# A gated attention and spectral mix on one core: another order list for all engines, another sequence of the last head groups

## The chip, the cores and the metric

The kernel runs on one core of one Trainium2 chip. The metric is device time in microseconds of one execution. A core has five engines that are written here as PE (TensorE, matrix products), ACT (ScalarE), DVE (VectorE), POOL (GpSimd) and SP (the queue that issues most DMAs). Each engine runs its instructions strictly in the order of its own queue and waits on semaphores where an operand comes from another engine. PE writes to PSUM, which here is cut into one place of three banks (psA), one of two (psB), one accumulator (pv) and two single banks (bg).

## What is computed

```
def _A_ref(x, wqkv, wo):                       # B, S, D = 1, 2048, 448; H = 16, Dh = 28
    qkv = (x @ wqkv).reshape(B, S, 3, H, Dh).transpose(2, 0, 3, 1, 4)
    q, k, v = qkv[0], qkv[1], qkv[2]
    p = softmax(einsum("bhqd,bhkd->bhqk", q, k) * Dh ** -0.5)
    o = einsum("bhqk,bhkd->bhqd", p, v)
    return o.transpose(0, 2, 1, 3).reshape(B, S, D) @ wo

def _B_ref(x, w_r, w_i):                       # a spectral filter over (S, D)
    X = rfft2(x) * (w_r + 1j * w_i)
    return irfft2(X, s=(S, D)).astype(bfloat16)

g = sigmoid((x * gate_w).sum(-1, keepdims=True))
return g * _A_ref(x, wqkv, wo) + (1 - g) * _B_ref(x, w_r, w_i)
```

Full softmax attention over 2048 tokens and 16 heads, mixed token by token with a two-dimensional Fourier filter of the same input.

## The kernel before

**Tiling.** The 16 heads are four groups g of four heads, each head on one strip of 32 partitions (28 used). The queries are four blocks c of 512. A pair (g, c) is a round n; there are 16 rounds, and `self.groups` (plan_steps) gives their sequence: groups 0 and 1 in order of c, then the eight pairs of `LAST8` (line 31) for groups 2 and 3. Within a round the keys are 16 tiles kt of 128.

**Scores and exps.** A unit is one (round, key tile, head): a 128x512 score product on one row strip of PE. Units are taken three and two at a time (`WID`), alternately into psA and psB; one such step is one score operation on PE and one exp on ACT (line 953, in attention()), which writes bf16 into a ring of 25 slots, or for the first eight spare steps into a pd tile. There are 315 steps. A score needs its PSUM place back from the exp two steps earlier. Beside the exps, the last four key tiles of most rounds are not given to ACT: their scores (called dunit) go to a bg bank, DVE turns each into a bf16 approximation of an exponential by an integer conversion (line 988, "conv"), and three further copies at other phases are made with one integer addition (line 1000, "phase"), each either by DVE or by POOL. A pv product (four column-tiled matrix products into the accumulator pv) takes each key tile's result.

**Rounds.** After a round's last pv product DVE copies the accumulator out, two small DMAs and one large broadcast through DRAM (rs, rsc, Rb) bring the reciprocal of the softmax sum times the gate to all rows, and POOL multiplies (line 1080, in normalise()); the result lies in q, whose block is no longer needed. An output tile t of 128 tokens (out_tile()) sums four products of the inverse transform and four of wo, one for each group g, of q's block c = t // 4; a tile can be finished when all four groups have that block normalised. The last round has a shorter path of its own (last_norm(), lines 1090 to 1114), and tiles 12 to 15 end with it.

**Everything else** is woven between the steps: the transposes of x, the q, k and v projections (mm4(), four column-tiled products), the forward transform, the filter product and the inverse transform (background()), all through the two bg banks.

**The head.** head() loads x and the first q and k weights, spreads those weights into padded tiles wpq and wpk (ACT copies, line 494; the borders are set by POOL memsets, lines 480 to 484, in padset()), transposes x on PE (line 425), copies the result to xT (DVE line 559, ACT line 557), projects q and k, and adds a row with the squared norms. `NWARM` = 14 products of a zero tile (set by a POOL memset, line 514) run on PE ahead of and among the first transposes.

**What sets the order.** Every operation is an Op object with an engine, a function that emits its instructions, its dependencies, and figures for its duration (dur) and latency (lat). The kernel has no scheduler: plan() reads the order from a table, `PLAN`, and issue() emits in that order. PLAN has three parts, two of them compressed: a list of operation numbers for all engines together (a number of 60000 or more is a filler, a warming product of zeros, see filler()); one byte for each PSUM item and pd tile that says which bank or buffer it takes; and a list of those phase operations that run on DVE rather than POOL (alts). Each engine's queue is the list restricted to that engine. The framework puts semaphores where the data demand them; issue() adds one wait of its own, from a DVE operation marked lk to the next POOL operation in the list.

```
def plan(self):
    order, place, alts = PLAN
    order = np.frombuffer(zlib.decompress(base64.b85decode(order)), "<u2")
    place = np.frombuffer(zlib.decompress(base64.b85decode(place)), "u1")
    for it, b in zip(self.items, place):
        it.bank = int(b)
    for i in alts:
        self.ops[i].eng = "DVE"
    return [int(i) if i >= 60000 else self.ops[i] for i in order]
```

Of the kernel before, what the change touches and what calls it, by code (L numbers as in the profile page):

```python
# [20 lines left out]
S, D, H, DH, F = 2048, 448, 16, 28, 225  # L21
F2 = 2 * F
NT, P, C = 16, 128, 112
# [7 lines left out]
LAST8 = [(2, 0), (2, 1), (2, 2), (3, 0), (2, 3), (3, 1), (3, 2), (3, 3)]  # L31
# [6 lines left out]
TA, TB, BREL = 40, 300, 26.0  # L38
XREL, WREL = (0.0, 6.0, 11.0), 30.0
EARLY = 8  # L40
KA = 256
PLAN = (
    (
        'c-kG8Qx_Ok&;YM?@9y5%wr$(CZQHhO+qRP;wr#et+c?dKA24Sg=ZsQDf$}PbBBhm8F;y&uDz<V;6sw@(s0b>qil{29$SR(SqN1w!'
        'Dw?XK5~!N0txBl6tE8%;s-@bgL~5K$p+>62Dw0a3lBiB9x$3M^snjZsN~zMRv?_y2uQI8Os;bJYqN^;by{e+Jsvatv%C2&#d@85P'
        'rE;r0DzD0~3aEmrwrZ>jsiLZwDy)jDBC3QcsY<ERs;o+GQkrrqg{h;;sPbx#nycoi3TnPus1~WkYJpm!E~`}Lin^+<smZE|TB=f;'
        'DJre0r_z|~YMENDR;ZP#zj~+Mt5vFn`k>O8(dwgGt<sy-@{d}hTB;0YfXZmrsy(Wj+N<`d{c4?BD+g3&vtCtKnanx0L7i6@)J3&j'
        't&$yTr@EwesVpX|StGmEG&Nn#k{N2I>aCipY^IsYZU(77YO0#8`l^kpz8a+(s7<Panx%%Q9A>kcAzM^VQ&$aDTh%u8o2sFHS6$Q}'
        'Dwp|F&5_*Zpt_-EN*<Hf98xz`R5`2~s#YqQZ={B)Tk43)XKt%W>W<29=E)aTz<gCJ<*xds3Yyj`nzT{()OR&jCHIBQeO1`3kRR%V'
        'I;o17@#>WNSDjV^)lt=4olz52QIo<CR$bLG)lC&Q#mreXTzyh$eMhxi>dI$T!qk&7s=hRkpK63EX%@PMa$HSNDSauk$jx=7O)5Xn'  # L50
        '&39!?S+l?`cIo^Q_du01<;^npm-<^hRm<H&^-NVT70pZ4PbvLaY5hVO{Z?6B$y7E@XYkKe6;su$a7$fR=_V^(cX^|FNJd}H^pxsm'
        'olET>sr4?sf2C@enr4+-<5s&gKC^$VviP;GmZ@zvyHt9UORdxBI;O7K;x@RnI;&5ox4L?!zS-t7`4|#Y8klVUiE3zex{WTD>~gUs'
        'yD#r6`Z&_a%$CMxyQ|=LxUzn(q}NSMWxv}sH3wV<{hQ0E_qa^DnQ3nRbeVNQU%<C82VG0^yDQ}Px<A~1s*3-mTA9{npDW|{yQ)5m'
        'Zez0QZ2FKp>Dn65<@_nv&K!2_O?I7A=h8WJ2a{Xp(MMfJlUEn^MSUl8#C0}B{4rPCcQMCZS3~-QV=X%99KM@5?Yf%?x|T2Q&$t@C'
        'hv{jqxQP0kyXqq8$U2JdWqO+nE~+l(EBQX=qU&p}xwEdizwS_%@Fl(1{Y-yz$<_3iT{InC4=^$Gc{k9+*0)?t9Y+r`adj*mPY*Wn'
        'bqsUY4K+hdHGj{Q_9OI2eZwV^QF^o<W)jOySIQ4JV{{U^?M9jrrj8%1hv=dDjvJ<X_)%uK{@aZ<&HYo?*^e<V+*p%9kJaP!cs)Un'
        'Gvm!m*Hd-z6ZJDU!L;<x-77cIH1n@rS3k+zcau#_^Uh7ull2rm#XN9R^;_4?Pt#M)L)YEMGSkc>H{JB~u}xcvV`i9k^2Eh8Gfh0x'
        '!asKLO?&AevrIz$mz!-8>BKsT?kI2EKtIRy^GWqw^RH{|6PQn~m7ixmyToR``RKm5gr=<@;1`%g<{!7vymu*dZ~wtnm1>eqSC>U5'
        'pI&TI>i)ilEHQQc54Y6Rl<%&MZ|8ry{JMZHs0-<3ri3o6mz)1wQT^4G)GN&jlT?c7Z?3OTCVhMn{mUhn6q3`gGQCtT?_sq`DeXN$'
        'aUEcd>E$CpL|AJ&_&h!mbn@%Wdc%<0#}$FRKAyyv4JLu)^BawUD3DN+nvUK=a;;#K*=#hF)#Y?~y~R|}0M&I3T~k-o`F$<D)zsG8'  # L60
        '%{G%)@`-~%KED)@tg^#olY%nXXO|o@%P;adWvAI~5O$eNGR8-Ru|BiR_i1I1spqpu9N25pNnDui(@O@~XG-h+roPW8sU$Kq@Z)`I'
# [12 lines left out]
        'PHX6wp9{I{Wyx)4!AzJ93*eIEv6>dbHOXt|L7@3?LN3YyIVt&UetSx;$Zz5(0xf~7Qoyc;g7$Y=1AoXPi9(kClnYYG7Pc$lu{_eJ'
        'WfeTuPjnHxR6mrWb}1}^zw}?S45HH+iAE2knEhK9w~JvpJdv}q0!r9(5{d51c`0cJ>g#et)<a|}WlP%)a8uSoMDkR|Mx~gv5#Grb'
        'C~JY<%T|a%<?K4x1m*1@9g8a1igp`(l+BQYGSFMu4u8v2S*&AIC3{OM+h>xLZcAp0E*Ytc-3fc4s@)AbB%?i$g?`Bn$VAzwn%xKg'
        '$Zt^H{thbCur=*|NJ$_32YD_B;EtrA<n+<+g1hpMuVri7KjEqVPoC*I_PM?%HoVXWp{{+YPrw^VO((&GdiDs^w>ju29D^6qz<%+^'
        ';Se;me?XHLpZ#HYDgXLc(#STpap<SKmbCQApMfT}sXYs+=p6hjr{R;Nq0e#|n%U+y59OjO(85Lz=b@!N1?lMmxDYWw$VvGLLo3_b'
        'UW9b?McUX)kT~3cuW}RaKwBF%<fW?+CES8`w!O_ww;>-z3SWJ8>R|7}J?Ll?gsgNQ_UUNBhyA*fEkK=ZT>2*Q=(}8l($vK!30>_&'
        'C_@p#0ev01+3xm-Jc8eJDf(Uau+O2VeF1+#e5yqW=x?C#7<$>>Hc_ZUPv8M?kdTP_*qRhV!qC?~g}U?%qKEjQ9QCsW=^ga9uOUV#'  # L80
        'PYLNg46qI9B~+uNA!c|318rHVM}zEJNFP4HVEYPc&_~D^{(&KOsQnlI&>6y?`k+3fGlgOH6AZW2sWu(fpCMToVUvdjlp>6@UtyFT'
        'ZNEW*P>E88CRCZm*e_5hjI}@E7gV6k;Xg=B6{$Yu4+_WG@fOizmhc^7g$Z_|{Q<GV5q(r2(*}?0Np`X&JfSr<qQ=A+Crq(%LlsIF'
        ';)SW!VZqRp04)kmv(s%=3V2eV(lhL7-HguYnf9zs75Y;jnq|-F$T-_(4Si{j%@#US6pV;-Z3oI8Qin8Qo}F*|QQA-;oYx&`fz1&v'
        '=!^Q2E<_bWOk8LS(`B7A6rorc0T<cDHab=cT`2}e#j;_EU23CYu8=#F51lAa_@v8(Wp=rJrOO2|!F<*$Z3$XoBVhznj3OE^XbOkO'
        'CN_FQW|fU(iqmS#CJ7d$q`1bewRuAqii7#W5E@98LtLy9*4gzo0aguPbvNokQOpKAls4Lg*gC|+K~$3BWBZT@H`&cLF{Z{2p%+yP'
# [162 lines left out]
class Kernel:  # L248
# [250 lines left out]
    def head(self):  # L499
        nc = self.nc  # L500
        self.grp = "head"
        K0 = -5000.0
        self.pad_ms, self.wready, self.d_x, self.xev, self.xtr = {}, {}, [], {}, []
        dx = [self.dma(self.xtok[:, 2 * i:2 * i + 2, 0:D], self.x[:, 2 * i:2 * i + 2, :], (), K0 + i, dur=0.5,
                       lat=3.2 + 0.4 * i, kb=224) for i in range(2)]
# [33 lines left out]
        trs = {}  # L539
# [820 lines left out]
```

## Time and profile before

| | |
|---|---|
| median of three runs | 385.3 us (385.23 to 385.51) |
| the profiled execution, its own time | 386.27 us |
| its span, first to last instruction | 384.5 us |
| granted TensorE clock, core 0 | 1.000 |
| bytes moved by DMA | 21.63 MB, mean 56 GB/s |

A profile line of a group reads: line, engine, operation, tile written <- tiles read, partitions x elements and type, count | busy time, mean ns of one | idle time of the engine before them, and what ended it. In a timeline the first two numbers are the start within the span and the length in us. PEld are PE's weight loads. Idle time of an engine that ends the moment an operand comes is shown as a wait for the engine that made it.

### The profile page before, as it was taken

The numbers are of one execution on the slowest core, as the hardware profiler recorded it, in microseconds if no ns is written. First come the engines' busy times: TensorE is split into PE (matmuls) and PEld (weight loads), VectorE is DVE, ScalarE is ACT, GpSimd is POOL, SyncE is SP. The second block draws the span as 40 slices with busy tenths as digits, with TensorE's granted clock in tenths as the row PEclk, the third lists the DMA queues.
The fourth block names the chain that finished last, engine by engine and source line by source line (L and its number), as shares of the span: only waits on it lengthen the run. The fifth ranks groups of instructions, "written<-read, shape, count | busy, mean of one in ns | idle before, by whom it ended". The sixth has DMA issues, their size and how long they took to land.

```text
span 384.5 us, 12127 instructions
## 1 busy us (share of the span) xinstructions
PE 369.8 (96%) x4994; PEld 143.6 (37%) x4994; DVE 337.8 (88%) x556; ACT 367.1 (95%) x333; POOL 229.1 (60%) x236
## 2 busy tenths in 40 slices
PE   8999999999999999999999999999999999999996
PEld 5543333334343334333333334333324423333343
DVE  2769998999899999999999999999999998878524
ACT  4899999999999999999999999999999999999992
POOL 4133756335766687778886876766667755842520
PEclk9999999999999999999999999999999999999999
DMA  8341000001230013233333113111123120020111
GB/s 225 93 129 47 9 2 2 14 7 46 56 102 11 2 51 82 69 74 74 86 86 86 37 31 95 44 42 34 38 71 104 56 67 14 4 82 26 55 38 61
DMA packets 31811, 21.63 MB, mean 56 GB/s; under 512 B 16572, under 2 KB 29596, under 8 KB 31756
## 3 DMA queue, kind: packets, MB, share of 16 engines
q1 hardware_dynamic: 30684, 20.54, 19.6%
q8 instruction: 39, 0.64, 0.7%
q10 hardware_dynamic: 1072, 0.32, 0.4%
q14 instruction: 16, 0.13, 0.1%
HBM read 14.97 MB, written 1.97 MB: 44 GB/s over the span
## 4 chain that ended last, share of the span: by engine, by line
PE 56%; DVE 18%; ACT 14%; issue 5%; DMA 3%; SPq 2%; POOL 0%; DVEq 0%; ACTq 0%; POOLq 0%
PE bg L417 27%; PE pvb L417 16%; ACT ring L953 14%; DVE pd L988 7%; PE psA L417 7%; PE psB L417 5%; DVE pd L1000 2%; DVE X L1292 2%; SPq L400 2%; DVE tt L1249 1%; PE bg L425 1%; DMA xtok<-Ab 1%; DVE sq L724 1%; DMA xtok<-in_A_x_dram 1%; DVE X L1198 1%
## 5 line engine op out<-in xcount | busy, mean ns | idle before, releaser
L953 ACT ACTIVATE ring<-psA 128x1536 bf16<-128x1536 f32 x154 | 227.8, 1479 | 3.4 <-PE psA L417 2.6
L1000 POOL TENSOR_SCALAR pd<-pd 128x2048 uint16<-128x2048 uint16 x84 | 158.9, 1898 | 81.9 <-DVE pd L1000 40.3
L953 ACT ACTIVATE ring<-psB 128x1024 bf16<-128x1024 f32 x153 | 161.5, 1055 | 1.6 <-PE psB L417 1.3
L988 DVE TENSOR_SCALAR pd<-bg 128x512 uint16<-128x512 f32 x236 | 156.0, 684 | 7.4 <-PE bg L417 3.8
L417 PE MATMUL bg<-q,k 32*128 32x512 bf16 x236 | 88.0, 380 | 3.9 <-DVE pd L988 2.1
L417 PE MATMUL pvb<-pd,vd 128*32 128x512 bf16 x944 | 85.8, 384 | 0.1
L417 PEld LDWEIGHTS <-k 32*128 32x128 bf16 x1024 | 37.5, 91 | 109.1 <-issue 103.7
L417 PE MATMUL pvb<-ring,vw 128*32 128x512 bf16 x768 | 71.7, 384 | 0.3 <-DVE pvs L1069 0.2
L417 PE MATMUL psA<-q,k 32*128 32x512 bf16 x474 | 63.8, 384 | 1.5 <-ACT ring L953 1.2
L1000 DVE TENSOR_SCALAR pd<-pd 128x2048 uint16<-128x2048 uint16 x93 | 63.7, 701 | 1.3
L417 PE MATMUL psB<-q,k 32*128 32x512 bf16 x314 | 63.3, 383 | 1.1 <-ACT ring L953 0.8
L417 PEld LDWEIGHTS <-vd 128*32 128x32 bf16 x944 | 23.6, 95 | 32.8 <-issue 26.8
L417 PEld LDWEIGHTS <-vw 128*32 128x32 bf16 x788 | 20.0, 95 | 30.7 <-issue 27.0
L1080 POOL TENSOR_TENSOR q<-pvs,Rb 128x512 bf16<-128x512 f32 x15 | 19.1, 1272 | 13.2 <-DVE pd L1000 9.7
L417 PEld LDWEIGHTS <-xT 112*128 112x128 bf16 (+1 forms) x512 | 19.6, 97 | 10.3 <-issue 6.7
L1249 DVE TENSOR_TENSOR tt<-bg,Wg 128x900 bf16<-128x900 f32 x16 | 17.4, 1091 | 1.3 <-PE bg L417 0.7
L417 PE MATMUL bg<-xT,wpk 112*32 112x512 bf16 (+2 forms) x252 | 18.3, 377 | 0.0
L866 POOL TENSOR_TENSOR vd<-vraw,wg 128x448 bf16<-128x448 f32 x16 | 15.0, 941 | 5.2 <-DVE pd L1000 4.9
L417 PE MATMUL bg<-xT,wpq 112*32 112x512 bf16 (+1 forms) x240 | 17.0, 382 | 0.2 <-DVE pd L988 0.2
L417 PE MATMUL bg<-wo,q 128*32 128x448 bf16 x236 | 17.1, 353 | 0.0
L1148 DVE CAST fin<-bg 128x448 bf16<-128x448 f32 x12 | 7.5, 623 | 10.5 <-PE bg L417 10.2
L417 PE MATMUL bg<-Bd,X 113*32 113x448 bf16 x240 | 16.6, 355 | 0.0
(123 smaller groups left out, 324.2 us busy)
## 6 DMA issues: line engine op xcount, KB each, us to landing
Rb<-rsc SPq DMA_DIRECT2D x60, 64.0 KB
CS<-cCS SPq DMA_DIRECT2D x16, 192.0 KB
Wg<-in_B_w_i_dram SPq DMA_DIRECT2D x64, 28.1 KB
xtok<-Ab SPq DMA_DIRECT2D x16, 112.5 KB
V<-xtok SPq DMA_DIRECT2D x16, 112.5 KB
xtok<-in_A_x_dram SPq DMA_DIRECT2D x3, 448.0 KB
out_dram<-fin SPq DMA_DIRECT2D x12, 112.0 KB
Wg<-in_B_w_r_dram SPq DMA_DIRECT2D x32, 28.1 KB
```

The source lines that it names most:

```text
L400: self.pin(e.dma_start(out=out() if callable(out) else out, in_=in_() if callable(in_) else in_))
L417: self.pin(self.nc.tensor.matmul(out, lhsT=lhsT, rhs=rhs, start=start, stop=stop, **kw))
L425: self.pin(self.nc.tensor.transpose(out=out, in_=in_, identity=self.ident[0:n, 0:n]))
L724: s = self.dve(0.065 + n / 1920.0, lambda: self.pin(nc.vector.tensor_tensor(out=self.sq[:, a:a + n], in0=T[:, a:a + n], in1=T[:, a:a + n], ...
L866: self.pin(nc.gpsimd.tensor_tensor(out=self.vd[g][:, f, :, :, 0:DH], in0=src, in1=wv, op=ALU.mult))
L953: self.pin(nc.scalar.activation(out=home[:, u0:u0 + len(st), :], in_=slot[:, 0:len(st), :], func=ACT.Exp, scale=LN2 / UNITS))
L988: self.pin(nc.vector.tensor_scalar(out=self.pd[y.bank][:, s, :].bitcast(U16), in0=self.bgi(it), scalar1=127 * UNITS, scalar2=0.0, op0=ALU. ...
L1000: self.pin(e.tensor_scalar(out=fl(self.pd[z.bank]), in0=fl(self.pd[y.bank]), scalar1=float(PHASE[f]), scalar2=1.0, op0=ALU.add, op1=ALU.mult))
L1080: e = self.pool(1.24, lambda: self.pin(nc.gpsimd.tensor_tensor(out=dst, in0=pvs[:], in1=self.Rb[:], op=ALU.mult)), ds, kk)
L1148: e = self.dve(0.55, lambda: self.pin(V.tensor_copy(out=fin, in_=bank())), [ops[-1], self.fdma[t % 2]], key, **a)
L1249: self.pin(nc.vector.tensor_tensor(out=tt[:], in0=free_dims(self.bgi(it), [[0, 2], [F, 2], [1, F]]), in1=free_dims(Wg[:], [[F, 2], [F, 2], ...
L1292: self.pin(nc.vector.tensor_tensor(out=free_dims(self.zt[0:FN], [[128, 4], [1, 128]], 512 * t), in0=self.bgi(it)[0:FN, :].rearrange("p (a ...
```

## The change

`PLAN` is replaced by another table of the same form. Decoded and compared engine by engine:

- The list has the same 2996 operations. It has 5 fillers where it had 11, all of the form "zeros added into pv".
- The list of phase operations on DVE has 85 entries where it had 93; POOL has 92 phases where it had 84.
- Every engine's queue is in another order, from the first instruction on. PSUM items and pd tiles are put into other banks and buffers.
- POOL's queue begins with memsets of wpq tiles (90, 110, 10), then zero (5), where it began with zero. The first 14 products of zeros on PE stand as 11 ahead of the transposes and 3 later (before: 12, then 2 among the transposes).

`LAST8` has the round (2, 3) as the last but one, where it was the fifth of the eight. In head() the latency of the first x loads and the duration of the first transposes are other numbers; these are annotations of the Op objects.

```diff
-LAST8 = [(2, 0), (2, 1), (2, 2), (3, 0), (2, 3), (3, 1), (3, 2), (3, 3)]
+LAST8 = [(2, 0), (2, 1), (2, 2), (3, 0), (3, 1), (3, 2), (2, 3), (3, 3)]
...
 PLAN = (
     (
-        'c-kG8Qx_Ok&;YM?@9y5%wr$(CZQHhO+qRP;wr#et+c?dKA24Sg=ZsQDf$}PbBBhm8F;y&uDz<V;6sw@(s0b>qil{29$SR(SqN1w!'
+        'c-jrp(*hXC4gk<(CX)<m+qP}nwr$(CZQJc`v8-*|wza+Y>HNT{2MPc>fd>N!8tQ{ULa>koDuaUr&;nw^5U2?8Au)7^7|<W$LOdWy'
...
-    [1185, 1186, 1187, 1198, 1207, 1218, 1220, 1231, 1240, 1251, 1252, 1253, 1264, 1273, 1274, 1285, 1286, 1306,
+    [1185, 1186, 1187, 1196, 1208, 1220, 1242, 1251, 1252, 1253, 1263, 1274, 1275, 1286, 1306, 1317, 1319, 1330,
...
         dx = [self.dma(self.xtok[:, 2 * i:2 * i + 2, 0:D], self.x[:, 2 * i:2 * i + 2, :], (), K0 + i, dur=0.5,
-                       lat=3.2 + 0.4 * i, kb=224) for i in range(2)]
+                       lat=3.55 + 0.4 * i, kb=224) for i in range(2)]
...
-                trs[i, c] = self.pe(0.13, f, [dx[i], d_id, msx] + ([trs[0, c]] if i else []), K0 + 10 + i + j * .1, **a)
+                trs[i, c] = self.pe(0.21, f, [dx[i], d_id, msx] + ([trs[0, c]] if i else []), K0 + 10 + i + j * .1, **a)
```

More of the change, by code (lines that the diff above doesn't have):

```diff
@@ new lines @@
+        '1d)LuCPaa#P!j@FfzHqyB0vg=2(=(NM1n5R5>i4mNCwd%6{LaGkPgy92B->2Aw6V*j8F+OLlzhbSs@o>gI16o8bChC0SzH1G=^A^'
+        '8}dUQC;)jO4)lbAPzZ`bVJHU0p$L?KIWQOIL0Om&$<+c#sZywtPzuUHX($8Zpgf$13s3<TLTy+Ci(v_*Qj=jRq*fPU3S5FZkVd6d'
+        'mth$!hZWEjn!rkk=HEa%wF=U!x&AG@gQ$KrWKi#6Dy)HO@BuQam3}S!4w=+$*aLf^2CRd9kXfzv>mjS^16kBG7y#R02keAZeiuxK'
+        '8Sop-gzAt@WmmJIHT(gCp(*?cvml3>1b@NbFdlNMe_(|_1*hQ*oP}KKU)TtvVH2E#%`n?<f!t~v%=CFx9<?8~!aRQk4!~7t1lM4W'
+        'zYbp@pV|O7U?AjIsbnamkeg6IO@xA~E!={3Fb3MdSNH~N{cZRT-Jp;vtd{#9&>oIJ2RI6Yposbi$KW^&gSv1KPQVObR5gQ?(h+9)'
```

121 lines of the change are left out of this document (58 added, 63 removed), and 17 rows, old and new, of the table PLAN.

## The prediction

> **What bounds the kernel now.** I read the page's busy shares first, then ScalarE's own timeline, then busy time by stretch, then who waits for whom.
>
> ```profile
> span 384.5 us, 12127 instructions
> ...
> PE 369.8 (96%) x4994; PEld 143.6 (37%) x4994; DVE 337.8 (88%) x556; ACT 367.1 (95%) x333; POOL 229.1 (60%) x236
> ...
> L953 ACT ACTIVATE ring<-psA 128x1536 bf16<-128x1536 f32 x154 | 227.8, 1479 | 3.4 <-PE psA L417 2.6
> ...
> L953 ACT ACTIVATE ring<-psB 128x1024 bf16<-128x1024 f32 x153 | 161.5, 1055 | 1.6 <-PE psB L417 1.3
> ```
>
> Three engines are near full. The order's own engine is ScalarE: 315 exps (eight go to pd), one after another.
>
> ```profile
> 10.29 1.45 ACT L953 ACTIVATE ring<-psA 128x1536 bf16<-128x1536 f32 x1 [0.73 <-PE psA L417]
> ```
> ```profile
> 190.70 1.49 ACT L953 ACTIVATE ring<-psA 128x1536 bf16<-128x1536 f32 x1
> 192.03 1.07 ACT L953 ACTIVATE ring<-psB 128x1024 bf16<-128x1024 f32 x1
> 192.94 1.51 ACT L953 ACTIVATE ring<-psA 128x1536 bf16<-128x1536 f32 x1
> ```
> ```profile
> 375.22 1.45 ACT L953 ACTIVATE ring<-psA 128x1536 bf16<-128x1536 f32 x1
> ```
> ```profile
> L812 ACT ACTIVATE w<-bg 128x16 f32<-128x16 bf16 (+1 forms) x7 | 1.6, 230 | 0.3 <-PE bg L425 0.3
> ```
>
> An undisturbed pair of exps takes 192.94 - 190.70 = 2.24 us. From the first exp's start to the last's there are 314 steps, 157 x 2.24 = 351.7 us; they took 375.22 - 10.29 = 364.9. So 13.2 us were lost, 1.6 of them to the small w exps. The rows show only 3.4 + 1.6 = 5.0 us of idle time, because an exp starts 0.16 us before its forerunner ends (190.70 + 1.49 against 192.03): a score up to that much late costs time without showing as idle. Some 11 us, then, are scores that came late. The span is 10.3 of head, 351.7 of exps, 13.2 lost, and 9.3 of tail.
>
> ```profile
> 10.30:50.00 39.70, 39.37 (x525) 17.52 (x525) 32.62 (x59) 39.03 (x38) 17.16 (x41) 1.00 0.25 65
> 50.00:100.00 50.00, 49.48 (x685) 18.49 (x683) 46.40 (x79) 48.85 (x45) 24.55 (x19) 1.00 0.07 15
> ...
> 200.00:250.00 50.00, 48.15 (x661) 18.51 (x660) 49.01 (x76) 49.91 (x45) 35.52 (x33) 1.00 0.23 57
> 250.00:300.00 50.00, 47.40 (x576) 17.32 (x575) 48.81 (x82) 49.99 (x45) 32.70 (x29) 1.00 0.20 59
> ...
> 345.00:376.70 31.70, 31.70 (x509) 12.46 (x503) 16.01 (x27) 30.32 (x27) 10.74 (x8) 1.00 0.13 40
> ```
>
> The columns are length, then PE, PE's weight loads, VectorE, ScalarE and GpSimd, then granted clock. ScalarE idles where PE is fullest (1.15 us in 50 to 100, 1.38 after 345) and hardly in between (0.01 in 250 to 300), where VectorE is the fuller one, 48.8 of 50.
>
> **What the change does, and what it costs.** Its three numbers in head() (the lat and dur arguments) cost nothing: they only annotate Op objects, and plan() reads the order from PLAN. The rest is a new list. I counted both lists engine by engine; instructions and bytes are the same, but for three things.
>
> First, the products. These rows give their prices.
>
> ```profile
> 345.49 0.39 PE L417 MATMUL psA<-q,k 32*128 32x512 bf16 x3
> 345.50 0.39 PE L417 MATMUL bg<-q,k 32*128 32x512 bf16 x1
> 345.81 0.40 PE L417 MATMUL pvb<-pd,vd 128*32 128x512 bf16 x4
> 346.04 0.39 PE L417 MATMUL pvb<-ring,vw 128*32 128x512 bf16 x4
> 346.25 0.36 PE L417 MATMUL bg<-Bd,X 113*32 113x448 bf16 x4
> 346.45 0.36 PE L417 MATMUL bg<-wo,q 128*32 128x448 bf16 x4
> 346.74 0.39 PE L417 MATMUL psB<-q,k 32*128 32x512 bf16 x2
> ```
> ```profile
> 380.61 0.38 PE L417 MATMUL bg<-wo,q 128*32 128x448 bf16 x4
> ```
>
> A column-tiled product of 512 holds PE for 346.25 - 346.04 = 0.21 us, one of 448 for 0.20. Going from row tiles (scores, and the products that VectorE converts) to column tiles, or back, adds 0.1: 345.49 to 345.81 is 0.32, 346.45 to 346.74 is 0.29. A score and a single product on another row strip run together (345.49 and 345.50). So the cost of an order is its own products, plus 0.22 for each row slot, plus 0.105 for each change of tiling. The old list has 348 slots and 610 changes, the new one 360 and 645: fewer single products stand beside a score. That is 12 x 0.22 + 35 x 0.105 = +6.3 us. Six of eleven warming fillers go (four products of 256 columns on four column strips, some 0.11 together): -0.7. Sum +5.6 us of PE.
>
> Where does it fall? For 25 exps ScalarE needs 12.5 x 2.24 = 28.0 us. PE's count for steps 40, 65, 90, 115, 140, 165, 190, 215, 240 and 265, 25 each, was 26.7, 28.3, 26.9, 24.3, 25.1, 24.3, 25.0, 23.0, 24.1, 26.7; it becomes 26.6, 28.7, 26.7, 26.2, 25.4, 25.8, 24.5, 24.5, 24.5, 27.3. Nearly all of it goes into the middle, under the exps that cover it; without that cover it would cost all 5.6. Being fuller still makes late scores likelier. The stretch 50 to 100 has hardly any room on PE and idles 1.15 us; 200 to 300 has some 4 us per 25 exps, so 7 per 50 us, and idles 0.05. That is 0.17 us of idle per us of room; lost time being 2.6 times what shows as idle (13.2 to 5.0), about 0.3 to 0.4, and I take 0.3: 5.6 x 0.3 = +1.7. The bounds are 0 and 5.6.
>
> Second, the waits. All background products go through two PSUM banks (bg), and PE, which works in order, stands until VectorE has emptied the bank; the next score stands behind it.
>
> ```profile
> PE bg L417 <- DVE pd L988: 2.5, 12, 0.3
> ```
> ```profile
> L988 DVE TENSOR_SCALAR pd<-bg 128x512 uint16<-128x512 f32 x236 | 156.0, 684 | 7.4 <-PE bg L417 3.8
> ```
> ```profile
> L1000 POOL TENSOR_SCALAR pd<-pd 128x2048 uint16<-128x2048 uint16 x84 | 158.9, 1898 | 81.9 <-DVE pd L1000 40.3 <-PE bg L417 20.9 <-DVE pd L988 8.4
> ```
> ```profile
> L1000 DVE TENSOR_SCALAR pd<-pd 128x2048 uint16<-128x2048 uint16 x93 | 63.7, 701 | 1.3
> ```
>
> A bank needs about 1 us from the end of its last product: 0.2 of pipeline, 0.68 of conversion and two hand-overs. I counted the PE work that each list puts between two uses of a bank. Below 1.0 us stood 144 of 404 uses, lacking 25.2 us in all; now 134, lacking 19.5. At 0.8 it is 42 against 34. So 5.7 us less standing, at the same 0.3: -1.7, with bounds -5.7 and 0. VectorE also gives eight phase operations to GpSimd: -8 x 0.70 = -5.6 us on an engine that is full from 100 to 300, +8 x 1.90 = 15.2 on one with 81.9 us of idle before such work. I price that at nothing beyond the -1.7; without GpSimd's idle time its consumers, the pv products, would wait up to 1.2 us each.
>
> Third, the head.
>
> ```profile
> 0.80 0.31 POOL L514 MEMSET zero<- 128x256 bf16 x1 [0.29 <-POOLq L1344]
> 1.17 2.74 PE L417 MATMUL psA<-zero 128*128 128x256 bf16 x12 [1.17 <-POOL zero L514]
> 2.89 0.20 POOL L484 MEMSET wpk<- 112x32 bf16 x2
> 4.12 0.56 ACT L494 COPY wpq<-X 112x448 bf16<-112x448 bf16 x1 [0.81 <-POOL wpk L481]
> 6.27 0.58 ACT L557 COPY xT<-psB 113x512 bf16<-113x512 bf16 x1 [1.58 <-PE psB L425]
> 6.75 0.57 ACT L494 COPY wpk<-X 112x448 bf16<-112x448 bf16 x1
> 7.46 0.60 PE L417 MATMUL bg<-xT,wpk 112*128 112x256 bf16 x4
> 7.56 0.60 ACT L593 ACTIVATE q<-psA 128x512 bf16<-128x512 f32 x1 [0.24 <-PE psA L417]
> ```
> ```profile
> L661 POOL MEMSET wo<- 128x448 bf16 x4 | 1.8, 476 | 0.5 <-DVE xT L687 0.5
> ...
> L649 POOL MEMSET vw<- 128x256 bf16 x2 | 0.6, 314 | 2.8 <-DVE sq L724 2.8
> ...
> L480 POOL MEMSET wpq<- 17x128 bf16 x4 | 0.8, 199 | 0.6 <-DVE xT L687 0.4
> ```
>
> GpSimd's first twelve operations, from zero to the last border of wpk, took 0.80 to 3.09. In the new list eleven of them come mixed with ten others before wpq's borders are done: two of wo, one of vw, four of 17x128, three tiny ones. That is about 2.1 + 2 x 0.48 + 0.31 + 4 x 0.20 + 3 x 0.11 = 4.5, with the gaps 4.7: wpq's borders end at 5.5, not 2.4, and wpk's at 6.0. ScalarE's queue there is copy wpq, copy wpk, copy xT, then q: it starts the first at 5.5 instead of 4.12, and at some 0.5 each copy xT ends near 7.15, not 6.85. Behind it stand the last two q products and the whole chain to the first score. +0.3, from 0 (the operations pack tighter) to the third rival's +1.3.
>
> Last, the tail. From the score at 345.49 to the last product at 380.61 PE needed 35.1 us; my count gives 34.5 and for the new list 33.8. PE's work beyond ScalarE's remaining exps, at its largest over all starting points, is 6.40 before and 6.33 now: -0.1, with bounds -0.7 and +0.8 (from the last seven exps on the new list is fuller, 14.4 against 13.6). The new group order only changes which head group's rows come late: the next-to-last round is normalised some 20 us before the end,
>
> ```profile
> 362.28 1.28 POOL L1080 TENSOR_TENSOR q<-pvs,Rb 128x512 bf16<-128x512 f32 x1 [3.50 <-DMA Rb<-rsc]
> ```
>
> and its first readers were output tile 8 (rows 3, 2), now tile 15 (rows 2, 3), which stands behind the score of step 312, one of the last three. So that wait gets longer cover, and I price it at nothing; without the cover it would cost what that normalisation is late.
>
> Sum: +1.7 - 1.7 + 0.3 - 0.1 = +0.2. The profiled execution took 386.27 with a span of 384.5, so 1.0 above the median of 385.3; as a difference the sum gives 384.7 for the span and **385.5** for the median.
>
> **The rivals.** One: the spacing pays fully. VectorE was the fuller engine in 200 to 300, and the terms of standing are real stops whereas fuller PE stretches have cover. Half of the 5.7 comes off the exps, and the head keeps +0.3: 382.8. Against it: ScalarE idles almost nowhere there, so there is little to win.
>
> Two, slower: the extra row slots decide, in steps 65 to 190, from the point where PE's count with its stops exceeds 28.0 per 25 exps; 28.7 exceeds it already without any. At half of 5.6, less 0.6 of waits, plus the head: 387.8. For it: 50 to 100 loses most today. Against: four counts in the middle stay below 26.
>
> [...]
>
> Four: the fillers did keep the clock up, and with five in place of eleven it falls. PE is busy 47.4 of 50 us at its emptiest, which speaks against it. Each us at half clock would cost about 0.7, since 24 of 28 become 48; one such lapse of 3 us gives 387.6.
>
> **How the numbers follow.** The forecast that the terms cancel has 0.45, its own range being 384.2 to 386.9; rivals one to four have 0.26, 0.19, 0.07 and 0.03. About 0.2%, 0.8 us, is what a measurement tells from no change: below 384.5 counts as faster, above 386.1 as slower. The forecast's share splits 0.09, 0.23 and 0.13, so faster 0.36 (0.09 + 0.26 and a hundredth), same 0.25, slower 0.39. The range reaches past both large rivals, 382.3 to 388.2.
>
> **What would show it.** Right: the first exp near 10.6, wpq's copy near 5.5, lost time between first and last exp within 1.5 of 13.2, the last product some 35 us after step 290's score. Rival one: lost time near 10. Rival two: idle before exps of over 2 us in 50 to 100, or any in 200 to 300. [...] Four: a granted clock below 1.00 between 190 and 310. I am wrong if the head begins as early as before, or if the loss changes by more than 3 us.

## The result, and the profile after

The changed kernel took 384.66 us (median of 15 runs, 383.52 to 385.47) against 385.48 us (median of 15, 385.21 to 385.83) for the kernel before: a ratio of 0.9978, 95% interval 0.997 to 0.9987. That is 0.8 us faster, where no change (385.5) was forecast. Timed twice more, beside the experiments, it gave 0.9971 (0.9941 to 1.0001) and 0.9943 (0.9925 to 0.996). Ratios compare fast runs alone, and a profiled execution at a lower granted clock (0.85 in one of those below) is not read.

The profiled execution took 383.52 us with a span of 381.7 us. It is the fastest of the 15, and the profiled execution of before (386.27, span 384.5) was slower than all of its 15 (385.83 at most). So of the 2.7 us between the two spans (384.46 - 381.73) only some 0.8 to 2.2 are in the ratios of the runs, and a second and a third profile were needed (below).

From the page of the changed kernel, the busy shares and the groups that answer to those shown before:

```profile
span 381.7 us, 12075 instructions
...
PE 370.6 (97%) x4970; PEld 143.3 (38%) x4970; DVE 334.8 (88%) x548; ACT 364.9 (96%) x333; POOL 243.9 (64%) x244
...
L952 ACT ACTIVATE ring<-psA 128x1536 bf16<-128x1536 f32 x154 | 237.0, 1539 | 2.8 <-PE psA L416 2.5
L999 POOL TENSOR_SCALAR pd<-pd 128x2048 uint16<-128x2048 uint16 x92 | 173.6, 1899 | 67.5 <-DVE pd L999 24.9
L952 ACT ACTIVATE ring<-psB 128x1024 bf16<-128x1024 f32 x153 | 170.6, 1115 | 1.8 <-PE psB L416 1.3
L987 DVE TENSOR_SCALAR pd<-bg 128x512 uint16<-128x512 f32 x236 | 156.2, 685 | 11.2 <-PE bg L416 6.6
...
L999 DVE TENSOR_SCALAR pd<-pd 128x2048 uint16<-128x2048 uint16 x85 | 58.2, 704 | 1.3 <-POOL rrg L1072 0.4
```

In sum eight phases went from DVE (93 to 85) to POOL (84 to 92). By the two lists it is 35 that went to POOL and 27 that came to DVE; the prediction had only the difference. DVE, which stood 7.4 us before its conversions, now stands 11.2, and PE hardly waits for them any more (us, times, longest; before, this line had 2.5, 12, 0.3):

```profile
PE bg L416 <- DVE pd L987: 0.6, 3, 0.2
```

DVE waits for PE instead of PE for it. The mean exp is longer (1479 to 1539 ns), but this is no slower engine: the time of an exp is counted from its start, and on average an exp now starts 0.17 us before its forerunner ends, where it was 0.10. ACT's idle time hardly moved (3.4 + 1.6 to 2.8 + 1.8 us). As in the prediction, the idle column does not show the lost time; the starts of the exps do. From ScalarE's timeline of the changed kernel, the first and the last:

```profile
10.18 1.45 ACT L952 ACTIVATE ring<-psA 128x1536 bf16<-128x1536 f32 x1 [0.85 <-PE psA L416]
...
372.26 1.45 ACT L952 ACTIVATE ring<-psA 128x1536 bf16<-128x1536 f32 x1
```

372.26 - 10.18 = 362.1, less the 351.7 of undisturbed exps: 10.4 us lost, where it was 13.2. So the span fell by 0.1 in the head and 2.85 in the exps, and gave back 0.2 in the tail (from the start of the last exp to the end 9.47 against 9.24). Busy time by stretch (length, PE, its weight loads, DVE, ACT, POOL, clock):

```profile
50.00:100.00 50.00, 49.73 (x686) 17.30 (x686) 45.88 (x78) 49.32 (x46) 29.22 (x20) 1.00 0.11 31
...
200.00:250.00 50.00, 49.11 (x672) 18.23 (x664) 49.09 (x78) 50.00 (x47) 38.89 (x35) 1.00 0.24 59
250.00:300.00 50.00, 47.72 (x567) 17.98 (x563) 48.28 (x79) 50.00 (x46) 38.10 (x31) 1.00 0.19 56
```

The granted clock is 1.00 in each of these stretches, so the missing fillers cost no clock there (rival four).

### The profile page after: what moved, and what is told of

Same layout as the page of the kernel before. It is cut to its first block, busy times and chain, and to the rows that moved or that the text cites. A ratio compares the mean times of both kernels' runs of the same rounds, so it can differ in the third digit from the quotient of the medians.

```text
span 381.7 us, 12075 instructions
## 1 busy us (share of the span) xinstructions
PE 370.6 (97%) x4970; PEld 143.3 (38%) x4970; DVE 334.8 (88%) x548; ACT 364.9 (96%) x333; POOL 243.9 (64%) x244
## 4 chain that ended last, share of the span: by engine, by line
PE 71%; ACT 11%; DVE 9%; issue 3%; DMA 3%; SPq 1%; POOL 1%; ACTq 0%; DVEq 0%; POOLq 0%
PE bg L416 33%; PE pvb L416 22%; ACT ring L952 10%; PE psA L416 9%; PE psB L416 7%; DVE pd L987 4%; DVE tt L1248 2%; PE bg L424 1%; DVE pd L999 1%; DMA X<-in_A_wqkv_dram 1%; SPq L399 1%; DVE X L1197 1%; DMA CS<-cCS 1%; DMA Wg<-in_B_w_r_dram 1%; DMA Wg<-in_B_w_i_dram 1%
## 5 line engine op out<-in xcount | busy, mean ns | idle before, releaser
L952 ACT ACTIVATE ring<-psA 128x1536 bf16<-128x1536 f32 x154 | 237.0, 1539 | 2.8 <-PE psA L416 2.5
L999 POOL TENSOR_SCALAR pd<-pd 128x2048 uint16<-128x2048 uint16 x92 | 173.6, 1899 | 67.5 <-DVE pd L999 24.9
L952 ACT ACTIVATE ring<-psB 128x1024 bf16<-128x1024 f32 x153 | 170.6, 1115 | 1.8 <-PE psB L416 1.3
L987 DVE TENSOR_SCALAR pd<-bg 128x512 uint16<-128x512 f32 x236 | 156.2, 685 | 11.2 <-PE bg L416 6.6
L416 PE MATMUL pvb<-pd,vd 128*32 128x512 bf16 x944 | 84.4, 384 | 0.3 <-POOL vd L821 0.2
L416 PEld LDWEIGHTS <-k 32*128 32x128 bf16 x1024 | 39.7, 91 | 108.7 <-issue 103.0
L416 PE MATMUL psA<-q,k 32*128 32x512 bf16 x474 | 62.6, 383 | 1.1 <-ACT ring L952 0.8
L416 PE MATMUL psB<-q,k 32*128 32x512 bf16 x314 | 61.8, 383 | 1.2 <-ACT ring L952 1.1
L999 DVE TENSOR_SCALAR pd<-pd 128x2048 uint16<-128x2048 uint16 x85 | 58.2, 704 | 1.3 <-POOL rrg L1072 0.4
L416 PEld LDWEIGHTS <-xT 112*32 112x32 bf16 (+1 forms) x512 | 19.6, 97 | 11.1 <-issue 7.5
L416 PE MATMUL bg<-Bd,xT 112*32 112x450 bf16 x256 | 16.9, 356 | 0.0
```

Source lines behind the costliest of these rows:

```text
L416: self.pin(self.nc.tensor.matmul(out, lhsT=lhsT, rhs=rhs, start=start, stop=stop, **kw))
L952: self.pin(nc.scalar.activation(out=home[:, u0:u0 + len(st), :], in_=slot[:, 0:len(st), :], func=ACT.Exp, scale=LN2 / UNITS))
L987: self.pin(nc.vector.tensor_scalar(out=self.pd[y.bank][:, s, :].bitcast(U16), in0=self.bgi(it), scalar1=127 * UNITS, scalar2=0.0, op0=ALU. ...
L999: self.pin(e.tensor_scalar(out=fl(self.pd[z.bank]), in0=fl(self.pd[y.bank]), scalar1=float(PHASE[f]), scalar2=1.0, op0=ALU.add, op1=ALU.mult))
```

## The experiments

The edits that follow change the list after it is decoded, in plan(), by lines like these; each text says which numbers.

```diff
+        order = [int(i) for i in order]
+        for i, j in AHEAD:              # move operation i ahead of j
+            order.remove(i)
+            order.insert(order.index(j), i)
+        for i in FILL:                  # a filler behind operation i
+            order.insert(order.index(i) + 1, 60000)
+        for i in TO_DVE:
+            self.ops[i].eng = "DVE"     # or TO_POOL, "POOL"
```

### Both kernels profiled again: what repeats

> The changed kernel itself, beside the three others on their chip: a second profile and the ratio there. Expected 0.998; if the profiled execution is again among the faster ones, its span is below that of before by 2 us or more, otherwise by about 1.

> The kernel before once more: a second profile. Expected from the pair of profiles of the changed kernel: behind step 92 the exps come at the same distances to 0.05 us, and only the head (first exp at 10.3 us in the first profile) and steps 0 to 8 differ.

> The changed kernel itself, on one chip with the run after it, because the two were never timed side by side. Theory H: ratio to before 0.9965 to 0.998, runs spread over 1.5 us or more, as in its first 15 runs (383.52 to 385.47). Rival Z (the gain seen with the constants' load first was the chip or luck): 0.9955, as the run after it.

The distances between the starts of exps, read from ScalarE's timeline of each profile, in us (steps 0, 8, 92, 184, 290 and 314; the last column runs from the start of the last exp to the end of the span):

| kernel, profile | first exp | 0-8 | 8-92 | 92-184 | 184-290 | 290-314 | tail |
|---|---|---|---|---|---|---|---|
| before | 10.29 | 9.96 | 98.41 | 106.62 | 120.85 | 29.08 | 9.24 |
| before, again | 10.06 | 9.97 | 98.43 | 106.09 | 121.19 | 29.08 | 9.24 |
| changed | 10.18 | 9.74 | 98.05 | 105.63 | 120.08 | 28.57 | 9.47 |
| changed, again | 10.90 | 10.83 | 98.05 | 105.64 | 120.08 | 28.58 | 9.48 |
| changed, third | 10.42 | 9.56 | 98.06 | 105.64 | 120.08 | 28.57 | 9.36 |
| changed, eight phases back on DVE | 10.71 | 9.56 | 98.92 | 106.57 | 120.97 | 28.58 | 9.76 |
| before, the eight phases on POOL | 10.34 | 9.97 | 100.73 | 107.54 | 122.50 | 29.08 | 9.25 |
| changed to step 184, then before | 10.78 | 9.56 | 98.06 | 105.94 | 121.60 | 29.08 | 9.22 |
| before to step 184, then changed | 9.82 | 9.97 | 98.41 | 107.52 | 119.89 | 28.59 | 9.91 |
| before, 32 gaps filled | 10.31 | 9.96 | 98.46 | 106.18 | 121.12 | 28.94 | 9.25 |
| changed, 48 fillers | 10.61 | 9.56 | 98.05 | 106.76 | 120.21 | 28.57 | 9.30 |
| changed, 18 scores ahead | 10.29 | 9.56 | 100.49 | 106.93 | 120.55 | 28.53 | 9.64 |
| before, 28 scores ahead | 10.23 | 9.97 | 101.84 | 108.77 | 122.24 | 29.51 | 9.24 |

From step 8 on the three profiles of the changed kernel, the last two from two chips, agree to 0.02 us (352.34, 352.35 and 352.36 in all). The kernel before had 354.97 and 354.79 and repeats less well than was expected: 0.5 and 0.3 us in two stretches. Most of that are single late loads, one in each profile (0.3 us at step 128 in the first, 0.2 at step 250 in the second):

```profile
PE bg L417 <- DMA xtok<-Ab: 0.3, 1, 0.3
```
```profile
PE bg L417 <- DMA V<-xtok: 0.2, 1, 0.2
```

With the shorter of the two for each stretch, before would have 354.4. The gain behind step 8 is 2.4 to 2.6 us in these executions, some 2.1 against that 354.4. What varies in the changed kernel is ahead of step 8. In the slower second profile of the changed kernel, PE and ScalarE:

```profile
9.14 0.39 PE L416 MATMUL pvb<-sq,cst 128*128 128x512 bf16 x1 [0.62 <-DMA cst<-ccst]
...
12.92 0.43 PE L424 MATMUL bg<-ident,xtok 128*113 128x128 bf16 x4 [1.06 <-DMA xtok<-in_A_x_dram]
```
```profile
10.90 1.45 ACT L952 ACTIVATE ring<-psA 128x1536 bf16<-128x1536 f32 x1 [0.85 <-PE psA L416]
...
21.73 1.46 ACT L952 ACTIVATE ring<-psA 128x1536 bf16<-128x1536 f32 x1
```

Two loads landed late: 0.7 us on the first exp, 1.1 us on the first eight steps. So the gain in the exps is real, and these three executions of the changed kernel differ by what the head does. That a median of only 0.8 us comes from more such heads is likely, but the other runs have no profile to show it.

### The phases

> The changed kernel with eight of its phase products, spread over rounds 1 to 13, moved back from POOL to DVE (93 phases on DVE as before), the order untouched. Theory D (the eight phases fewer on DVE are what emptied the bg banks sooner): the standing for DVE at a bank rises from 12.6 us toward 22, and the time comes back to about 385.5. Theory W (the order of bank uses shortened the waits, the phases play no part; the prediction priced them at nothing): standing within 2 us of 12.6 and the time within 0.3 us of 384.65.

The eight are one phase each of eight key tiles (TO_DVE = 1207, 1240, 1285, 1362, 1517, 1572, 1647, 1735), all on DVE before and on POOL in the changed kernel. They are eight of the 35 that went to POOL; the other 27, and the 27 that came to DVE, stay as the changed kernel has them. 386.81 us, ratio to before 1.0029 (1.0017 to 1.0042); the changed kernel on that chip had 0.9971 (0.9941 to 1.0001), so they cost 0.0058, 2.2 us. Its page, and a line of its waits:

```profile
L958 ACT ACTIVATE ring<-psA 128x1536 bf16<-128x1536 f32 x154 | 233.3, 1515 | 3.5 <-PE psA L422 3.0
L1005 POOL TENSOR_SCALAR pd<-pd 128x2048 uint16<-128x2048 uint16 x84 | 158.6, 1899 | 80.5 <-DVE pd L1005 36.5
L958 ACT ACTIVATE ring<-psB 128x1024 bf16<-128x1024 f32 x153 | 167.0, 1091 | 2.7 <-PE psB L422 1.9
...
L1005 DVE TENSOR_SCALAR pd<-pd 128x2048 uint16<-128x2048 uint16 x93 | 63.5, 701 | 1.3 <-POOL rrg L1078 0.4
```
```profile
PE bg L422 <- DVE pd L993: 3.1, 10, 0.6
```

POOL and DVE are back at their old counts, and ACT's idle at 3.5 + 2.7. From step 8 the exps take 355.04 us, all of the gain and a little more is gone, 0.9 us in each of the three long stretches. I also counted PE's standing from the trace (start of each operation less the moment at which the array was free by the prices of the prediction, where the last to be ready was DVE's reading of the bg bank): 22.5 us before, 12.6 changed, 17.3 here.

The trace shows the eight places one by one. The first row has the step in which each of the eight phases starts on DVE, the second what the ten steps from there take longer than in the changed kernel, in us:

| step | 32 | 46 | 68 | 107 | 173 | 201 | 229 | 266 |
|---|---|---|---|---|---|---|---|---|
| longer by | 0.44 | 0.21 | 0.28 | 0.58 | 0.38 | 0.32 | 0.11 | 0.40 |

Together they make 2.7 us, all of what the exps take longer (355.04 against 352.34). The first place, with the phase on DVE and then in the changed kernel:

```profile
49.62 0.68 DVE L1005 TENSOR_SCALAR pd<-pd 128x2048 uint16<-128x2048 uint16 x1
...
50.21 1.28 DVE L993 TENSOR_SCALAR pd<-bg 128x512 uint16<-128x512 f32 x2
...
50.95 1.05 PE L422 MATMUL bg<-xT,wpq 112*32 112x512 bf16 x16 [0.41 <-DVE pd L993]
51.93 0.39 PE L422 MATMUL psB<-q,k 32*128 32x512 bf16 x2
...
52.42 1.02 ACT L958 ACTIVATE ring<-psB 128x1024 bf16<-128x1024 f32 x1 [0.20 <-PE bg L422]
```
```profile
49.35 0.69 DVE L987 TENSOR_SCALAR pd<-bg 128x512 uint16<-128x512 f32 x1
...
50.12 1.05 PE L416 MATMUL bg<-xT,wpq 112*32 112x512 bf16 x16
...
51.10 0.39 PE L416 MATMUL psB<-q,k 32*128 32x512 bf16 x2
...
51.74 1.06 ACT L952 ACTIVATE ring<-psB 128x1024 bf16<-128x1024 f32 x1
```

The conversion starts behind the phase, PE stands 0.41 us for the bank, the sixteen q products and the score behind them come later, and the exp is 0.33 us late (the exps ahead of it are 0.35 apart in the two profiles, this one 0.68).

> The kernel before with the same eight phase products moved from DVE to POOL (85 on DVE, as in the changed kernel), its order untouched. Theory D (fewer phases on DVE are the gain, whatever the order; putting the eight back into the changed kernel raised the standing at bg banks from 12.6 to 17.3 us and cost about 1.9 us): standing falls from 22.5 toward 18, ratio to before about 0.996 to 0.998. Theory C (the place of each phase is worth something only with the order that was searched with it): ratio 0.9995 or above, POOL's later phases show up as PE or DVE waiting for POOL.

391.71 us, ratio 1.0181 (1.012 to 1.0242): 5.9 us slower, standing 26.4 us. Two lines of its waits (before, the first was 2.5, 12, 0.3 and the second is not there), and PE and ScalarE at one of the eight phases:

```profile
PE bg L423 <- DVE pd L994: 4.0, 15, 0.9
PE pvb L423 <- POOL pd L1006: 2.4, 3, 1.1
```
```profile
215.25 0.61 PE L423 MATMUL pvb<-pd,vd 128*32 128x512 bf16 x8 [1.06 <-POOL pd L1006]
...
216.32 1.02 ACT L959 ACTIVATE ring<-psB 128x1024 bf16<-128x1024 f32 x1 [1.08 <-PE psB L423]
```

Here the pv products stand where the old order has them, a phase takes 1.90 us on POOL instead of 0.70, and the score stands behind the product that waits. From seven of the eight phases on, ten steps take 0.6 to 1.1 us longer than in the second profile of before. Theory D falls, C stands: the same eight phases on POOL gain with the one order and lose with the other. These eight are worth nothing without the order, and the order nothing without them. What the exchange of the other 27 does was not tested.

### The two halves

The lists joined at the score of step 184: the first kernel's up to there, then what remains in the second's sequence, with the second's `LAST8`. The kernels of these runs hold the joined tables; the rule, in short:

```
head = first[:first.index(score184)]
order = head + [i for i in second if i not in head]
```

> The changed kernel's order up to the score of step 184, from there the order of the kernel before, with its interleaving of the last rounds. Theory W (the gain comes with the standing at bg banks, which fell by 4.9 of 9.9 us ahead of step 184): about half of the 0.8 us, 385.1. Rival L (the new interleaving of the last two head groups brings it): no gain, 385.5. Rival H (the head and the first rounds bring it): the whole gain, 384.65.

> The order of the kernel before up to the score of step 184, from there the changed kernel's order with its interleaving of the last rounds: the mirror of the run before it. Theory W: 385.1 (standing falls by the 5.0 of 9.9 us that lie behind step 184). Rival L: the whole gain, 384.65. Rival H: none, 385.5. If the two halves add up, the two mirrors' gains together make 0.8 us.

385.83 us, 1.0001 (0.9991 to 1.0011), and 385.29 us, 0.9982 (0.9969 to 0.9996). By time, the gain is in the second half; rival H, head and first rounds, falls. (The mirror's profile has 107.52 in steps 92 to 184, 0.4 of it at step 127 and 0.4 at the seam.) By the table, the first half brings 0.4 us in steps 8 to 92 as well, and gives it back at the seam (121.60 where before had 121.02 on average). Steps 290 to 314 take 28.6 us with the changed ending and 29.1 with the old one, whichever half comes ahead: 0.5 us. Whether the new sequence of the head groups or the new order of the output tiles there earns them was not separated.

### Filling PE's gaps

```diff
+AHEAD = [
...
+    (2332, 1718),      # a pv ahead of a dunit that waits for its bank
...
```

> The kernel before with 32 ready pv products moved ahead of an operation that PE stood before, waiting for DVE to empty its bg bank (7.2 us of standing at these places in the profiled execution, of which the 32 products fill 5.9); PE's work, the phases and all the other engines' orders stay. Theory W (standing of PE at bg banks costs 0.3 us of time per us, wherever the work comes from that fills it): -1.8 us, ratio 0.995. Rival (a pv filled in there was no loss where it stood, PE's standing there is covered by the two scores ahead): ratio within 0.999 to 1.001.

> The changed kernel with nine ready pv products moved ahead of operations that wait for a bg bank (2.1 us of standing, 1.8 of it filled). Theory W: -0.5 us against the changed kernel, ratio to before 0.9965. Rival: 0.998 as the changed kernel itself.

0.9998 (0.9981 to 1.0014) and 0.9966 (0.9942 to 0.9989, the changed kernel beside it 0.9971). Nothing was gained, so theory W falls in the form in which the prediction used it, a price for standing wherever the work comes from that fills it. From the waits of PE in the kernel before with its gaps filled (engine, line, waited for: us, times, longest):

```profile
PE bg L428 <- DVE pd L999: 1.8, 9, 0.2
PE psA L428 <- ACT ring L964: 1.4, 5, 0.5
...
PE psB L428 <- ACT ring L964: 1.2, 5, 0.3
```

Before, they were 2.5, 1.2 and 0.8: where the 32 products had stood, PE now waits for the exps to release a score's place. By my count, standing at banks went from 22.5 to 21.9 us and standing before scores from 8.6 to 10.7. So the 5.9 us that were filled came back as standing elsewhere, and these gaps were no loss: PE had that time to spare. What less standing in all is worth, this run cannot say.

### What a microsecond of PE costs

> The changed kernel with 48 more fillers (each four 256-column products of zeros into the pv bank, about 0.11 us of TensorE together), each right behind a pv that is neither the first nor the last of its round, between steps 115 and 265: 48 x 0.11 = 5.3 us more PE work in the middle, nothing else changed. Theory P (the term of the prediction: 0.3 us of time per us of PE work): +1.6 us, 386.2. Rival N (PE work in the middle lies in time in which PE would stand anyway, so it costs nothing): within 0.3 us of the changed kernel, 384.4 to 384.9. Rival F (every us of PE work is paid): +5.3, 389.9.

385.58 us, 0.9991 (0.9982 to 1.0001), so 0.0020 or 0.8 us over the changed kernel on that chip (0.9971, with an interval too wide to tell this from nothing by time); the exps from step 8 take 1.25 us more, in many small steps. 5.3 us of PE work cost 0.15 to 0.24 us each, between N and P.

```diff
+AHEAD = [
...
+    (799, 428),        # the score of step 126 ahead of the v products
...
```

> The changed kernel with 18 scores between steps 20 and 298, each over 0.1 us late behind products that began after its slot was free, moved ahead of these products (5.5 us of lateness in the two profiles, the same to 0.02 us in both); nothing else is moved. Theory S (time is lost where products stand between the release of a slot and its score, not where PE stands at a bank nor by PE's sum): the loss between exps in these steps falls by 2 to 5 us, ratio to before 0.985 to 0.993. Rival P (PE is as full as it can be, so lateness only goes to the next score): ratio 0.996 to 0.999.

> The kernel before with 28 late scores between steps 20 and 298 moved ahead in the same way (7.5 us of lateness). Theory S: the loss between exps falls by 3 to 7 us, ratio 0.982 to 0.993, below the changed kernel. Rival P: ratio 0.999 to 1.001.

A score is late where products stand between the release of its place and itself. The largest case of the changed kernel, step 126, in its timeline of PE and ACT:

```profile
154.74 1.55 ACT L952 ACTIVATE ring<-psA 128x1536 bf16<-128x1536 f32 x1
155.53 1.04 PE L416 MATMUL bg<-xT,wpq 112*32 112x512 bf16 x16
...
156.07 1.13 ACT L952 ACTIVATE ring<-psB 128x1024 bf16<-128x1024 f32 x1
...
156.51 0.96 PE L416 MATMUL bg<-wvr,xT 112*128 112x112 bf16 x16
...
157.40 0.39 PE L416 MATMUL psA<-q,k 32*128 32x512 bf16 x3
...
157.90 1.45 ACT L952 ACTIVATE ring<-psA 128x1536 bf16<-128x1536 f32 x1 [0.70 <-PE psA L416]
```

The exp that holds psA starts at 154.74 and lasts 1.55, so the place is free at 156.29; the sixteen v products go first, and the exp comes 0.9 us late (157.90 - 154.74 - 2.24). Scores over 0.05 us late behind such products were 55 in the first profile before and 38 in the changed kernel; 9.2 of its 9.4 us of lateness have PE busy all that time. Moving 18 of them ahead took 387.51 us, 1.0043 (1.003 to 1.0055); moving 28 in the kernel before 393.44 us, 1.0196 (1.0182 to 1.021). Both theories missed. The moves break pairs of row products and add changes of tiling: 24 changes and 9 row slots, 24 x 0.105 + 9 x 0.22 = 4.5 us of PE, and the exps from step 8 took 356.50 - 352.35 = 4.15 us more; 47 and 15, 8.2 us, cost 362.35 - 354.88 = 7.5. Here PE work costs 0.9 us per us, four times the fillers. The two prices are the prediction's, worked out from its rows (345.49 to 345.81, a row slot and a change of tiling, is 0.32 us).

> The changed kernel with the constants' load first, and 21 more fillers (0.11 us of PE each, 2.3 us in all, no further change of tiling), each put ahead of the row products that end in a score which was late (steps 22 to 283). Theory K (a microsecond of PE work costs all of itself where the score behind it is late, and nothing where PE stands before the next release anyway): +2 us, the exps' loss between steps 20 and 298 rises from 7.5 to 9.3 or more. Rival A (PE work has one average price, 0.2 by the 48 fillers, 0.3 by the prediction): +0.5 to +0.7 us.

> The same kernel with 21 fillers, the same 2.3 us, each put where PE stood 0.11 to 0.28 us (for a slot or for a bg bank) and none of the next scores was late. Theory K: within 0.3 us of the kernel without them. Rival A: +0.5 to +0.7 us, like the run before it.

> The changed kernel with the constants' load first once more, as the reference beside the two runs with fillers. Expected 0.9955 again, exps behind step 8 at the same distances to 0.05 us.

384.52 us, 0.9956 (0.9941 to 0.9971), for the reference; 385.65 us, 0.9989 (0.9976 to 1.0002), with 21 fillers ahead of late scores; 385.02 us, 0.9971 (0.9959 to 0.9983), ahead of covered ones. The same 2.3 us cost 1.1 in the one place and 0.5 in the other, with intervals that touch: the place seems to count, and by time not all or nothing as K says. In the second, the way from the first exp to step 184 was within 0.2 us of the reference's; behind it stood a wait for a late load, at the products of step 197, and one of an output copy for a late store, which PE and the exp of step 308 waited for in turn:

```profile
PEld L427 <- DMA CS<-cCS: 0.9, 1, 0.9
```
```profile
363.61 0.62 DVE L1158 CAST fin<-bg 128x448 bf16<-128x448 f32 x1 [1.66 <-DMA out_dram<-fin]
```

The exps lose 0.7 us at each of the two. That is 1.4 of the 1.63 us that they take longer from step 8 on (354.04 against 352.41), so in this execution the 2.3 us of covered fillers cost some 0.2, nearer to K than the medians.

### The constants' load

One edit, AHEAD = [(4, 79)]: the constants' load, fifth on SP's queue in the changed kernel, third before. The mirror is AHEAD = [(79, 4), (77, 4)].

> The changed kernel with the load of the constants ahead of the third x load and the gate weights on SP's queue (issued near 1.8 us, as before, not at 2.9). In the second profile of the changed kernel the product of the squares with the constants waited for that load until 9.14 us, and the first exp began at 10.90; in the first one 8.44 and 10.18. Theory H (the late constants cost the changed kernel part of its gain, and make its runs differ by 2 us): first exp near 10.2, time 0.4 to 0.8 us less than the changed kernel's beside it, ratio to before 0.9955, runs within 1 us. Rival (the third x load, now half a us later, is late in its place, or the lateness was covered): ratio 0.997 to 0.998.

> The kernel before with the third x load and the gate weights ahead of the constants on SP's queue, as the changed kernel has them: the mirror of the constants' test. Theory H: the constants are issued near 2.9 us, their first product waits for them, the first exp comes 0.3 to 0.8 us later, the time rises by 0.4 to 0.9 us (ratio 1.001 to 1.0025) and the runs differ by 1.5 us or more. Rival (the head of the kernel before has room for it, its squares are ready later): ratio 0.9995 to 1.0005.

> The changed kernel with the constants' load first, beside it. Theory H: 0.4 us or more below the changed kernel, ratio to before 0.995 to 0.996. Rival Z: within 0.2 us of it.

383.82 us, 0.9953 (0.9939 to 0.9966), looked like a gain of 0.8 us. The mirror spoke against it: 385.60 us, 0.9992 (0.9981 to 1.0002). Side by side the changed kernel had 383.86 us and this one 384.23, 0.9957 (0.9941 to 0.9973). Theory H falls: its first two numbers, from 5 and 7 runs, were set against the changed kernel on other chips. The last profile shows another reason for a late head. The q products in it, and in the changed kernel beside it:

```profile
6.61 1.81 PE L423 MATMUL psA<-xT,wpq 112*128 112x512 bf16 x4
8.25 0.27 PE L423 MATMUL psB<-xT,wpk 112*128 112x256 bf16 x1
8.36 0.60 PE L423 MATMUL bg<-xT,wpk 112*128 112x256 bf16 x4
```
```profile
6.22 1.21 PE L416 MATMUL psA<-xT,wpq 112*128 112x512 bf16 x4
```

In the first, products of 512 columns are 0.41 us apart ((8.25 - 6.61) / 4), against 0.21 in the prediction's rows, and from 8.25 on 256 columns take 0.11 (8.36 - 8.25). In the second that pace is there from 5.44 on, where the pairs of transposes come 0.11 us apart in place of 0.21:

```profile
4.36 0.42 PE L424 MATMUL pvb<-ident,xtok 128*113 128x128 bf16 x2
4.57 0.42 PE L424 MATMUL bg<-ident,xtok 128*113 128x128 bf16 x2
...
5.44 0.28 PE L424 MATMUL psB<-ident,xtok 128*113 128x128 bf16 x2
5.55 0.28 PE L424 MATMUL pvb<-ident,xtok 128*113 128x128 bf16 x2
```

The first product starts at 1.72 in both, and the first exps began at 11.40 and 10.42, 1.0 us apart. By the pace of the products that is rival three, a full clock that comes late, in one execution; the load that was moved may have a part in it.

## Why the prediction was wrong

**The failed step is the price of the phases, "at nothing beyond the -1.7".** The exps took 2.85 us less in the first pair of profiles, and 2.4 to 2.6 less from step 8 on, where the prediction's terms for them came to nothing. With eight of the phases back on DVE and the rest of the change in place, the exps from step 8 on take 355.04 us, as in the kernel before (354.97 and 354.79), and the time is 2.2 us longer than the changed kernel's. So the rest did cancel, as forecast, and what was forecast at nothing carries the gain, though only together with the order: in the old order the same eight cost 5.9 us. A phase on DVE holds the conversion behind it for 0.70 us, the bank stays full, and PE's work arrives where a score should stand; the first place above shows this chain, and all eight the late exps behind it. The wait that the prediction named for the pv products (up to 1.2 us) is what the old order meets (1.06). And the prediction took the difference of the two lists, eight, for the change; 35 phases went and 27 came.

**The waits' size.** Standing fell not by 5.7 but by 9.9 us (22.5 to 12.6). With the eight phases back it is 17.3, 5.2 less than before, about what the static count gave for the order. It took every emptying of a bank at 1 us and left out what else is in DVE's queue at that moment: the phases.

**The rate of 0.3.** It priced PE's 5.6 us of added work at "5.6 x 0.3 = +1.7" and 5.7 us less standing "at the same 0.3: -1.7", and let them cancel. (The working gives 0.17 x 2.6 = 0.44, not "0.3 to 0.4"; since both terms have the same rate, the sum stays.) That they do cancel within 0.3 us with the phases back (0.6 against the 354.4 above) is luck as far as the rate goes, for neither quantity has one: filling 5.9 us of gaps gained nothing, and PE work cost 0.15 to 0.24 us per us in fillers, 0.5 ahead of late scores and 0.9 where scores were moved. What the new list's 35 additional changes cost where they stand was not measured.

**The head.** Expected were the wpq copy near 5.5 and the first exp near 10.6. From the changed kernel's timeline:

```profile
4.07 0.56 ACT L493 COPY wpq<-X 112x448 bf16<-112x448 bf16 x1 [0.70 <-DMA X<-in_A_wqkv_dram]
...
5.19 0.20 POOL L483 MEMSET wpq<- 112x32 bf16 x2
```

The copy starts ahead of the borders: the listed dependency is only a dependency of the list, the semaphores follow the data, and borders and copied columns do not overlap. The borders themselves end at 5.4, near the 5.5 that was forecast; what failed is the wait for them. No cost of the late borders shows: the first exp comes at 10.18 and 10.42, and at 10.90 with the late load, against 10.29 and 10.06 before. The +0.3 was not there, and a head that begins as early as before is one of the prediction's own signs of being wrong. No run shows the further 1.0 us in the upper end of the head's range (+1.3) for the changed kernel itself: its first product came at 1.72 instead of 1.17, but its pairs of transposes start 0.11 us apart from 5.38 on (5.38, 5.49, 5.61), where before they are still 0.21 apart at 5.87. What the runs showed is the one execution with the constants first, at this pace only from 8.25 on, its first exp 1.0 us later than the changed kernel's beside it.

**The tail.** -0.1 was forecast; it is +0.1 to 0.2 behind the last exp, and 0.5 us won in the last 24 steps, which the prediction had not separated.

**The rivals.** Rival one gave 382.8, half of the standing off the exps and lost time near 10: lost time was 10.4, and 10.2 in the third profile (372.34 - 10.42 - 351.7), so it had the size of what the exps gain, by luck: it left the phases out, and its 382.8 is 1.9 us below the median. Rival two (row slots decide) and four (fillers and clock) did not come; three (a late full clock) came in one execution, with the constants first.

## What to carry to other kernels

Do not price a full engine's work or its waiting by an average rate: ask at each place what stands between the release of a buffer and the work that the bounding engine waits for. A gap that is filled has gained nothing until the bounding engine starts earlier. Ask the same of an operation that only changes engine: look at what stands behind it in the queue that it leaves, and who waits for it in the queue that it joins. When an order and an assignment of engines were searched together, test them together: half of the change can be worth less than none.

## What the hardware showed that was not expected

- Behind the head the changed kernel repeated to 0.02 us in 352 over three executions, so where two profiles of such a stretch agree, they settle a tenth of a us that medians of 15 runs cannot. One alone does not: with the constants first, the same list took 352.36, 352.41 and 352.94 us from step 8 on. The exceptions that the traces name are late loads: 0.9 us at step 197 above, and in the kernel before with its constants late a wait of 1.0 us, at the products of the forward transform:

```profile
PE bg L424 <- DMA xtok<-Ab: 1.0, 1, 1.0
```

- The clock fell to half for 3.4 us behind a wait. In the changed kernel with nine gaps filled, PE waited 1.39 us for a load until 13.29 us, and the granted clock was 0.50 from 13.3 to 16.7 and 1.00 on both sides (PE and the clock by stretch):

```profile
13.29 0.68 PE L432 MATMUL bg<-ident,xtok 128*113 128x128 bf16 x4 [1.39 <-DMA xtok<-in_A_x_dram]
```
```profile
6.50:13.30 6.80, 5.28 (x42) 2.96 (x41) 3.54 (x9) 4.05 (x6) 1.71 (x8) 1.00 1.05 265
13.30:16.70 3.40, 3.40 (x25) 2.36 (x25) 0.97 (x2) 1.07 (x3) 0.13 (x1) 0.50 0.84 155
16.70:20.00 3.30, 3.22 (x44) 1.21 (x43) 2.30 (x5) 2.98 (x4) 0.49 (x3) 1.00 0.50 129
```
```profile
9.90:13.30 3.40, 2.02 (x22) 1.00 1.10 222
```

In the 3.4 us ahead of the fall PE was busy for 2.02. The first eight steps took 12.65 us in place of 9.56. What made the clock fall is not shown.
